# Two-scale attention and an ELU MLP on one core: batch 0 on fp16 runs, masked by TensorE; batch 1 inside block 0

## The chip, the cores and the metric

One core of a Trainium2 chip runs the whole program: TensorE (PE, matmuls), ScalarE (ACT), VectorE (DVE), GpSimd (POOL), each with its own instruction queue, worked off in order, and the queue of SyncE (SP), which issues DMAs. The metric is the device time of one execution in microseconds (us), less is better.

## The reference

Attention on q, k, v of shape 8 x 8 x 576 x 64 (batches, heads, tokens, width), twice: once with tokens averaged in fours, once with every token seeing its neighbours within 3. The sum, as 4608 tokens of 512, feeds a two-layer MLP (512 to 2048 to 512) with an ELU. The factor is 4; k and v are averaged like q.

```python
def sm_attn(qq, kk, vv):
    s = scale * np.matmul(qq, kk.transpose(0, 1, 3, 2))
    ...
    return np.matmul(a, vv)
q_d = q.reshape(B, H, Sd, factor, D).mean(axis=3)
...
out_d = sm_attn(q_d, k_d, v_d)
out_up = np.repeat(out_d, factor, axis=2)
...
mask = np.abs(pos[:, None] - pos[None, :]) < factor
scores = scale * np.matmul(q, k.transpose(0, 1, 3, 2))
scores = np.where(mask, scores, -1000000000.0)
...
return (out_up + out_local).astype(np.float32)
...
h = x @ w_in
alpha = 1.0
g = np.where(h > 0.0, h, alpha * (np.exp(np.minimum(h, 0.0)) - 1.0))
return (g @ w_out).astype(np.float32)
```

## The kernel before

**Tiling.** Attention works on a pair of heads at a time (4 pairs a batch, 8 batches), and within a pair on 6 chunks of 96 tokens; the two heads stand on partitions 0 to 63 and 64 to 127. The MLP works on 9 blocks of 512 tokens. A batch has 576 tokens, so block t needs batches up to t, and blocks 7 and 8 have no attention beside them.

**A pair.** `load` brings q by a casting DMA from GpSimd (fp32 to fp16, runs of 64 numbers) and k and v as fp32 from SP, each with a halo of 3 rows at both sides in two small DMAs. `cast` (GpSimd) makes k and v fp16. `transposes` multiplies q and k with an identity that has the means' columns beside it, so that transposed q and k and their means come from the same matmuls, and the means of v go into the same tile; ACT evicts them as qt and kt, DVE as vd and kd. `scores` makes the local scores (96 columns a chunk) and the coarse ones (two groups of 72 keys); ACT takes their exponentials (pex, dex), and DVE multiplies pex with a 0/1 mask (mex).

**A batch.** `denominators` sums mex and dex by matmuls with an indicator, DVE takes reciprocals (rc). They are spread over partitions by a write to DRAM and four reads (`spread_out`, `spread_in`, issued by ACT), in batch 0 by matmuls (`spread_pe`). `outputs` multiplies with v; DVE scales (gn, ln) and GpSimd adds the two scales into xt, the MLP's input.

**The MLP.** `mm1(t, fc)` is one of 16 groups of four matmuls of 512 columns into hp; then ACT takes exp(hp) (e), DVE min(e, 1) - 1, and DVE max(hp, 0) + e, written to gt. `mm2(t, i)` adds four matmuls to a tile op; after four of them ACT copies op to os, and SP stores it.

**Memory of results (PSUM).** 8 banks of 2 KB a partition: pool "two" (2 tiles of 2 banks: tq, tk, sc, rb, lg), pool "hp" (2 tiles of a bank) and pool "misc" (2 tiles of a bank: den, op; in blocks 0 and 1 every other hp too).

**Order.** Every call stands in a list with a time (`at`), sorted by it, and this is the order on every engine's queue. A slot is one unit of this time, with one mm1 and one mm2. `start_of` gives mm1 of block 0 slots 0 to 15, mm2 of block 0 slots 16 to 31, mm1 of block 1 slots 32 to 47; from there mm1 of block t runs beside mm2 of block t-1. Batch b starts 26.5 slots ahead of its block, with the offsets in SLOTS.

Of the kernel before, what the change touches and what calls it, by code (L numbers as in the profile page):

```python
# [12 lines left out]
AF = mybir.ActivationFunctionType  # L13

B, H, S, D = 8, 8, 576, 64
SD = S // 4
SCALE = 0.125
QB, KW, NB = 96, 102, 6
HB = 3 * QB
QW, KWW = QB + 24, 24 + KW  # L20
# [9 lines left out]
def _np_consts():  # L30

    off = np.concatenate([np.arange(96), np.arange(-3, 0), np.arange(96, 99)])
    m = np.zeros((KW, NB, QB), dtype=np.float16)
    for c in range(NB):
        for u in range(QB):
            ok = (np.abs(off - u) < 4) & (off + QB * c >= 0) & (off + QB * c < S)
            m[ok, c, u] = 1.0
    r = np.zeros((KW, 24), dtype=np.float16)
    r[np.arange(96), np.arange(96) // 4] = 0.25
    qi = np.concatenate([np.eye(96, dtype=np.float16), r[:96]], axis=1)  # L40
    ki = np.concatenate([r, np.eye(KW, dtype=np.float16)], axis=1)
    vr = np.zeros((KW, 120), dtype=np.float16)
    vr[:, 48:72] = r
    indl = np.zeros((128, 37), dtype=np.float16)
    indl[:, 5] = 1.0
    seed = np.zeros((2, 32 + HB), dtype=np.float16)
    seed[0, 6:32] = 1.0
    seed[1, 4:6] = 1.0
    seed[0, 32:] = 1.0
    seed[1, 32 + SD :] = 1.0  # L50
    sel = np.zeros((NPAIR, 32, 3, 2, 64), dtype=np.float16)
    for e in range(2):
        for g in range(2):
            sel[:, 2 * e + g, g, e] = 1.0
        sel[:, 4 + e, 2, e] = 1.0
    return m, qi, ki, vr, indl, seed, sel.reshape(128, 384)
# [12 lines left out]
def kernel(  # L69
# [13 lines left out]
    ctx.enter_context(nc.allow_low_precision("fp16 operands of TensorE"))  # L83

    def const(a, name):
        t = sb.tile(list(a.shape), FP16, tag=name, bufs=1, name=name)
        nc.sync.dma_start(out=t[:], in_=nc.inline_tensor(a, name=name + "c").ap())
        return t

    def two(name):  # L90
        return ps.tile([128, 2, 512], FP32, tag="two", bufs=2, name=name)

    m_np, qi_np, ki_np, vr_np, ind_np, seed_np, sel_np = _np_consts()
    QI, KI = const(qi_np, "QI"), const(ki_np, "KI")
    consts = {}

    def late_consts():
        consts["VR"] = const(vr_np, "VR")
        consts["MASK"] = const(m_np, "MASK")
        consts["IND"] = const(ind_np, "IND")  # L100
        consts["SEED"] = const(seed_np, "SEED")
        consts["SEL"] = const(sel_np, "SEL")

    WI = sb.tile([128, DMC, DFF], FP16, tag="WI", bufs=1, name="WI")
    WO = sb.tile([128, FCN, DM], FP16, tag="WO", bufs=1, name="WO")

    def load_weights(i):

        if i < 8:
            src = moe_w_in.rearrange("(c p) m -> p c m", p=128)[:, :, 256 * i : 256 * i + 256]  # L110
            to = WI[:, :, 256 * i : 256 * i + 256]
        else:
            n = 2 * (i - 8)
            src = moe_w_out.rearrange("(c p) m -> p c m", p=128)[:, n : n + 2, :]
            to = WO[:, n : n + 2, :]
        nc.gpsimd.dma_start(out=to, in_=src)


    st16, stT, stB, stS, stR = {}, {}, {}, {}, {}

    st32 = {}

    def load(b, j):
        q16 = sb.tile([QB, 2, NB, 64], FP16, tag="q16", bufs=5, name="q16")
        k32 = sb.tile([KW, 2, NB, 64], FP32, tag="k32", bufs=3, name="k32")
        v32 = sb.tile([KW, 2, NB, 64], FP32, tag="v32", bufs=3, name="v32")

        def rows(src, c0, nblk, tok, n):
            a = src[b, 2 * j]
            blocks = [[QB * D, 2 * NB]] if nblk == NB else [[S * D, 2], [QB * D, nblk]]  # L130
            return bass.AP(
                tensor=a.tensor, offset=a.offset + (QB * c0 + tok) * D,
                ap=[[D, n], *blocks, [1, D]],
            )

        nc.gpsimd.dma_start(out=q16[:], in_=rows(q, 0, NB, 0, QB))  # L136
        for src, dst in ((k, k32), (v, v32)):
            nc.sync.dma_start(out=dst[0:96], in_=rows(src, 0, NB, 0, QB))
            lo = 1 if (b, j) == (0, 0) else 0
            hi = NB - 1 if (b, j) == (B - 1, NPAIR - 1) else NB  # L140
            if lo or hi < NB:
                nc.gpsimd.memset(dst[96:KW, :, 0 if lo else NB - 1, :], 0.0)
            for c0, nblk, tok, p in ((lo, NB - lo, -3, 96), (0, hi, QB, 99)):
                to, a = dst[p : p + 3, :, c0 : c0 + nblk, :], rows(src, c0, nblk, tok, 3)
                if nblk == NB:
                    nc.sync.dma_start(out=to, in_=a)
                else:
                    for e in range(2):
                        nc.sync.dma_start(out=to[:, e], in_=a[:, e])
        st32[(b, j)] = (q16, k32, v32)  # L150

    def cast(b, j):
        q16, k32, v32 = st32.pop((b, j))
        k16 = sb.tile([KW, NB, 2, 64], FP16, tag="k16", bufs=2, name="k16")
        v16 = sb.tile([KW, NB, 2, 64], FP16, tag="v16", bufs=8, name="v16")
        nc.gpsimd.tensor_copy(out=k16[:], in_=k32[:].rearrange("p e c d -> p c e d"))  # L156
        nc.gpsimd.tensor_copy(out=v16[:], in_=v32[:].rearrange("p e c d -> p c e d"))  # L157
        st16[(b, j)] = (q16, k16, v16)


    def transposes(b, j):
        q16, k16, v16 = st16.pop((b, j))
        VR = consts["VR"]
        tq, tk = two("tq"), two("tk")
        for c in range(NB):
            for e in range(2):
                nc.tensor.matmul(  # L167
                    tq[64 * e : 64 * e + 64, c // 3, QW * (c % 3) : QW * (c % 3) + QW],
                    q16[:, e, c, :], QI[:], start=True, stop=True,
                )  # L170
        for c in range(NB):
            nc.tensor.matmul(  # L172
                tq[0:KG, c // 3, 3 * QW : 3 * QW + 128],
                VR[:, 48 - 24 * (c % 3) : 120 - 24 * (c % 3)], v16[:, c, :, :],
                start=(c % 3 == 0), stop=(c % 3 == 2),
            )
        qt = sb.tile([128, 2, 3 * QW], FP16, tag="qt", bufs=2, name="qt")
        nc.scalar.copy(out=qt[:], in_=tq[:, :, 0 : 3 * QW])  # L178
        vd = sb.tile([KG, 2, 128], FP16, tag="vd", bufs=8, name="vd")
        nc.vector.tensor_copy(out=vd[:], in_=tq[0:KG, :, 3 * QW : 3 * QW + 128])  # L180
        for c in range(NB):
            nc.tensor.matmul(  # L182
                tk[:, c // 3, KWW * (c % 3) : KWW * (c % 3) + KWW], k16[:, c, :, :], KI[:],
                start=True, stop=True,
            )
        tk4 = tk[:, :, 0 : 3 * KWW].rearrange("p g (c w) -> p g c w", w=KWW)
        kt = sb.tile([128, 2, 3, KW], FP16, tag="kt", bufs=2, name="kt")
        nc.scalar.copy(out=kt[:], in_=tk4[:, :, :, 24:KWW])  # L188
        kd = sb.tile([128, 2, 3, 24], FP16, tag="kd", bufs=2, name="kd")
        nc.vector.tensor_copy(out=kd[:], in_=tk4[:, :, :, 0:24])  # L190
        stT[(b, j)] = (qt, kt, kd, vd, v16)


    def scores(b, j):
        qt, kt, kd, vd, v16 = stT.pop((b, j))
        sc = [two("sc"), two("sc")]
        for c in range(NB):
            for e in range(2):
                r = slice(64 * e, 64 * e + 64)
                nc.tensor.matmul(  # L200
                    sc[e][0:KW, c // 3, QB * (c % 3) : QB * (c % 3) + QB],
                    kt[r, c // 3, c % 3, :],
                    qt[r, c // 3, QW * (c % 3) : QW * (c % 3) + QB],
                    start=True, stop=True,
                )
        for kg in range(2):
            for e in range(2):
                r = slice(64 * e, 64 * e + 64)
                qd = _free(qt[r, 0, QB : QB + 1], [[QW, NB], [1, 24]])
                nc.tensor.matmul(  # L210
                    sc[e][0:KG, kg, HB : HB + SD],
                    _free(kd[r, 0, 0, 0:1], [[1, SD]])[:, KG * kg : KG * kg + KG], qd,
                    start=True, stop=True,
                )
        pex = sb.tile([KW, 2, S], FP16, tag="pex", bufs=2, name="pex")
        dex = sb.tile([KG, 2, 2, SD], FP16, tag="dex", bufs=8, name="dex")
        for e in range(2):
            nc.scalar.activation(  # L218
# [269 lines left out]
```

## Time and profile before

| what | value |
|---|---|
| three runs | 396.29, 398.57, 398.7 us |
| median | 398.57 us |
| profiled execution, span from first to last instruction | 396.9 us |
| mean granted TensorE clock | 0.991 |
| PE busy | 354.1 us (89%), 3244 matmuls |
| DVE busy | 244.8 us (62%) |
| ACT busy | 203.8 us (51%) |
| POOL busy | 136.6 us (34%) |

For the profiled execution the page gives its span, and no time of its own; the span lies within the three runs. The page cuts the span into 40 slices of 9.9 us, with a digit for the busy tenths of each. A group's line has the source line, the engine, the operation, output and inputs, their shapes and the count; then busy us and mean ns of one; then the idle time ahead of it and what ended it. A busy PE counts the modelled end of a matmul, some 0.17 us behind the last column, so times of matmuls in a row are read from start to start.

### The profile page before, as it was taken

Reading aid. Unit: us, or ns where it says so; the run is one execution under the profiler, and the core shown is the slowest. Engines: PE = TensorE matmul, PEld = TensorE weight load, DVE = VectorE, ACT = ScalarE, POOL = GpSimd, SP = SyncE. Lnnn points to the kernel's source line nnn. Section 1 sums busy time; section 2 is a strip of 40 time slices with the busy share of each in tenths; the row PEclk is TensorE's granted clock in tenths of the full one; section 3 lists DMA queues with packets and bytes.
Section 4 is the critical chain, followed back from the end, with each engine's and each line's share of the span. In section 5 each row is a group of like instructions: output and inputs, shape, how many; then the busy total and the mean of one; then the engine's idle time right before and its main releaser. Section 6 shows DMA issues by size and latency. Waiting matters only on the chain.

```text
span 396.9 us, 8379 instructions
## 1 busy us (share of the span) xinstructions
PE 354.1 (89%) x3244; PEld 183.9 (46%) x3244; DVE 244.8 (62%) x460; ACT 203.8 (51%) x377; POOL 136.6 (34%) x184
## 2 busy tenths in 40 slices
PE   0465699996987899999999999999999899999995
PEld 0343344553544455545555554555544444444442
DVE  0123578643697976877697769766977575555510
ACT  1363158643675475657556664666375334444421
POOL 4375694402930860383038204800520040000000
PEclk9999999998998999999999999999999999999999
DMA  9899999728996892997399439906401400101112
GB/s 125 154 187 176 182 191 183 106 25 167 202 125 146 168 85 55 206 196 48 79 229 168 31 96 226 168 2 138 122 26 36 129 28 26 54 26 38 43 53 80
DMA packets 138083, 44.91 MB, mean 113 GB/s; under 512 B 122580, under 2 KB 133436, under 8 KB 138044
## 3 DMA queue, kind: packets, MB, share of 16 engines
q1 hardware_dynamic: 85644, 29.79, 31.9%
q0 software_dynamic: 43776, 8.92, 25.9%
q10 hardware_dynamic: 8624, 5.68, 6.5%
q8 instruction: 25, 0.41, 0.5%
q14 instruction: 14, 0.11, 0.1%
HBM read 43.33 MB, written 9.95 MB: 134 GB/s over the span
## 4 chain that ended last, share of the span: by engine, by line
PE 77%; DVE 6%; ACT 5%; DMA 4%; ACTq 2%; issue 2%; POOL 1%; SPq 1%; POOLq 0%; DVEq 0%
PE op L384 30%; PE hp L364 28%; PE sc L200 4%; PE tq L172 3%; PE tq L167 3%; DMA v<-in_v_dram 3%; PE lg L321 3%; DVE gt L373 2%; ACTq L272 2%; PE tk L182 2%; ACT pex L218 2%; DVE e L370 1%; DMA rd<-rc 1%; DVE mex L228 1%; POOL xt L348 1%
## 5 line engine op out<-in xcount | busy, mean ns | idle before, releaser
L364 PE MATMUL hp<-xt,WI 128*128 128x512 f16 x576 | 150.1, 388 | 2.5 <-POOL xt L348 1.4
L384 PE MATMUL op<-WO,gt 128*128 128x512 f16 x576 | 145.8, 382 | 0.0
L369 ACT ACTIVATE e<-hp 128x512 f16<-128x512 f32 x144 | 85.6, 601 | 106.2 <-PE hp L364 96.3
L373 DVE SCALAR_TENSOR_TENSOR gt<-hp,e 128x512 f16<-128x512 f32 x144 | 99.6, 692 | 5.4
L370 DVE TENSOR_SCALAR e<-e 128x512 f16<-128x512 f16 x144 | 55.9, 388 | 53.1 <-ACT e L369 52.0
L364 PEld LDWEIGHTS <-WI 128*128 128x128 f16 x576 | 54.4, 99 | 68.4 <-issue 9.3
L384 PEld LDWEIGHTS <-gt 128*128 128x128 f16 x576 | 54.4, 98 | 63.5 <-issue 1.8
L156 POOL CAST k<-k 102x768 f16<-102x768 f32 x32 | 26.8, 836 | 95.1 <-DMA k<-in_k_dram 54.0
L348 POOL TENSOR_TENSOR xt<-ln,gn 128x512 f16<-128x512 f16 (+7 forms) x64 | 42.1, 689 | 46.9 <-DVE ln L339 46.9
L218 ACT ACTIVATE pex<-sc 102x576 f16<-102x576 f32 x64 | 41.4, 647 | 21.8 <-PE sc L210 21.6
L228 DVE TENSOR_TENSOR mex<-pex,MASK 102x1152 f16<-102x1152 f16 x32 | 26.2, 817 | 38.6 <-ACT pex L218 38.4
L157 POOL CAST v<-v 102x768 f16<-102x768 f32 x32 | 29.7, 927 | 37.3 <-DMA v<-in_v_dram 37.2
L178 ACT CAST qt<-tq 128x720 f16<-128x720 f32 x32 | 24.3, 758 | 35.3 <-PE tq L172 31.2
L390 ACT COPY os<-op 128x512 f32<-128x512 f32 x36 | 21.2, 588 | 19.9 <-PE op L384 19.9
L200 PE MATMUL sc<-qt,kt 64*102 64x96 f16 x384 | 18.9, 224 | 12.9 <-ACT kt L188 7.2
L180 DVE CAST vd<-tq 72x256 f16<-72x256 f32 x32 | 13.4, 417 | 27.5 <-ACT qt L178 26.5
L136 POOL DMA_DIRECT2D q<-in_q_dram x32 | 28.6, 893 | 3.9 <-DMA WI<-in_moe_w_in_dram 3.0
L167 PE MATMUL tq<-QI,q 96*64 96x120 f16 x384 | 17.4, 230 | 10.4 <-DMA q<-in_q_dram 5.9
L200 PEld LDWEIGHTS <-kt 64*102 64x102 f16 x384 | 14.0, 132 | 27.1 <-ACT kt L188 13.2
L222 ACT ACTIVATE dex<-sc 72x288 f16<-72x288 f32 x64 | 25.8, 404 | 0.0
L172 PE MATMUL tq<-v,VR 102*72 102x128 f16 x192 | 18.0, 234 | 7.0 <-POOL v L157 7.0
L339 DVE TENSOR_TENSOR ln<-lg,rcb 128x576 f16<-128x576 f32 x32 | 23.9, 746 | 0.0
(35 smaller groups left out, 211.9 us busy)
## 6 DMA issues: line engine op xcount, KB each, us to landing
k<-in_k_dram SPq DMA_DIRECT2D x32, 288.0 KB
v<-in_v_dram SPq DMA_DIRECT2D x32, 288.0 KB
out_dram<-os SPq DMA_DIRECT2D x36, 256.0 KB
q<-in_q_dram POOLq DMA_DIRECT2D x32, 144.0 KB, 4.5
rcb<-rd ACTq DMA_DIRECT2D x14, 288.0 KB
WI<-in_moe_w_in_dram POOLq DMA_DIRECT2D x8, 256.0 KB, 10.8
WO<-in_moe_w_out_dram POOLq DMA_DIRECT2D x8, 256.0 KB, 9.3
rcb<-rd ACTq DMA_DIRECT2D x14, 72.0 KB
```

Source lines behind the costliest of these rows:

```text
L157: nc.gpsimd.tensor_copy(out=v16[:], in_=v32[:].rearrange("p e c d -> p c e d"))
L167: nc.tensor.matmul(tq[64 * e : 64 * e + 64, c // 3, QW * (c % 3) : QW * (c % 3) + QW], q16[:, e, c, :], QI[:], start=True, stop=True,)
L172: nc.tensor.matmul(tq[0:KG, c // 3, 3 * QW : 3 * QW + 128], VR[:, 48 - 24 * (c % 3) : 120 - 24 * (c % 3)], v16[:, c, :, :], start=(c % 3 = ...
L200: nc.tensor.matmul(sc[e][0:KW, c // 3, QB * (c % 3) : QB * (c % 3) + QB], kt[r, c // 3, c % 3, :], qt[r, c // 3, QW * (c % 3) : QW * (c % ...
L218: nc.scalar.activation(out=pex[:, e, :].rearrange("p (g u) -> p g u", g=2), in_=sc[e][0:KW, :, 0:HB], func=AF.Exp, scale=SCALE,)
L228: nc.vector.tensor_tensor(out=mex[:], in0=pex[:], in1=mk2, op=AB.mult)
L348: nc.gpsimd.tensor_tensor(out=xt(t)[:, j, t0 - TBLK * t : t1 - TBLK * t], in0=ln[:, a:z], in1=_rep4(gn[:, a // 4 : z // 4]), op=AB.add,)
L364: nc.tensor.matmul(hp[:], WI[:, dc, 128 * fc : 128 * fc + 128], x[:, dc, :], start=(dc == 0), stop=(dc == DMC - 1),)
L369: nc.scalar.activation(out=e[:], in_=hp[:], func=AF.Exp)
L370: nc.vector.tensor_scalar(out=e[:], in0=e[:], scalar1=1.0, scalar2=-1.0, op0=AB.min, op1=AB.add)
L373: nc.vector.scalar_tensor_tensor(out=gts[t][:, fc, :], in0=hp[:], scalar=0.0, op0=AB.max, in1=e[:], op1=AB.add)
L384: nc.tensor.matmul(op_[:], gts[t][:, fc, 128 * tt : 128 * tt + 128], WO[:, fc, :], start=(fc == 0), stop=(fc == FCN - 1),)
```

## The change

**Batch 0** (`first_batch`, written out in order). q and k come by eight casting DMAs from GpSimd in runs of six tokens (1536 bytes of fp32), so that chunk c holds tokens 6r + c, and the eviction puts them in order by a strided read. The mask is added by TensorE: a matmul of an identity with -30000 or 0 goes into the scores' bank first. The means of q and k are reductions on DVE. The denominators are made in two halves of two pairs each (`den_half`), and spread by matmuls.

**Later batches.** q and k stay fp32, come from SP, are transposed as fp32 by TensorE, and evicted as fp16; their sums over four tokens are two steps of additions on GpSimd each. v comes with its halo in one DMA of 112 rows.

`den_half` has two seeds, 24 matmuls of 96 columns and 8 of 144; a half goes on with the sums of v, the spread and the outputs of its two pairs.

**Order.** mm1 of block t runs in slots 16t to 16t+15, mm2 of block t one block later, from block 0 on. Batch 1's attention stands within block 0, its outputs at slot 15.9. The loads of W_out are issued behind batch 0's outputs, those of W_in among batch 0's casts of v.

**PSUM.** The pools "hp" and "misc" are replaced by two tiles of two banks, duo0 and duo1. From block 1 on hp is one of duo0's halves in turn, op and den one of duo1's; in block 0 hp goes duo0, duo1, duo0, duo1. In batch 0 they hold the scores, half of the denominators and outputs.

```diff
+    duo = [ps.tile([128, 1024], FP32, tag=f"duo{i}", bufs=1, name=f"duo{i}") for i in range(2)]
...
+    def bank(i, n=512):
+        return duo[i // 2][:, 512 * (i % 2) : 512 * (i % 2) + n]
+
+    def misc_bank():
+        misc[0] += 1
+        return bank(2 + misc[0] % 2)
...
     def denominators(b):
-        den = ps.tile([128, 512], FP32, tag="misc", bufs=2, name="den")
+        den = misc_bank()
...
     def mm1(t, fc):
-        tag = "misc" if t < 2 and fc % 2 else "hp"
-        hp = ps.tile([128, TBLK], FP32, tag=tag, bufs=2, name="hp")
+        hp = bank((0, 2, 1, 3)[fc % 4]) if t == 0 else bank(fc % 2)
...
     def mm2(t, i):
-            ops[t] = ps.tile([128, DM], FP32, tag="misc", bufs=2, name="op")
+            ops[t] = misc_bank()
...
+    def load_qk(b, j):
+        for src, name in ((q, "q"), (k, "k")):
+            a = src[b, 2 * j]
+            if b == 0:
+                t = sb.tile([QB, 2, TPP * D], FP16, tag=name + "in", bufs=4, name=name + "16")
+                nc.gpsimd.dma_start(
+                    out=t[:],
+                    in_=bass.AP(
+                        tensor=a.tensor, offset=a.offset,
+                        ap=[[TPP * D, QB], [S * D, 2], [1, TPP * D]],
+                    ),
+                )
+            else:
+                t = sb.tile([QB, NB, 2, D], FP32, tag=name + "in", bufs=4, name=name + "32")
+                for e in range(2):
+                    nc.sync.dma_start(
+                        out=t[:, :, e, :],
...
...
+    def transposes(b, j):
...
+                if b == 0:
+                    for e in range(2):
+                        nc.tensor.matmul(
+                            t[64 * e : 64 * e + 64, 128 * c : 128 * c + QB],
+                            x[:, e, D * c : D * c + D], C["NI"][0:QB, 0:QB],
+                            start=True, stop=True,
+                        )
                 else:
+                    a = 512 * (c // 3) + QB * (c % 3)
+                    nc.tensor.transpose(
+                        t[:, a : a + QB], x[:, c, :, :].rearrange("p e d -> p (e d)"), C["I32"][:]
+                    )
...
+    def sums(b, j, x):
...
+        if b == 0:
+            nc.vector.tensor_reduce(
+                out=to[:], in_=src.rearrange("p (g f) -> p g f", f=4), axis=AX.X, op=AB.add
+            )
+        else:
+            two_ = sb.tile([128, 2 * SD], FP32, tag="t2", bufs=2, name="t2")
+            at_ = src.rearrange("p (g f) -> p f g", f=2)
+            nc.gpsimd.tensor_tensor(out=two_[:], in0=at_[:, 0], in1=at_[:, 1], op=AB.add)
+            at_ = two_[:].rearrange("p (g f) -> p f g", f=2)
+            nc.gpsimd.tensor_tensor(out=to[:], in0=at_[:, 0], in1=at_[:, 1], op=AB.add)
...
+    def den_half(b, h, den):
...
+        rc = RC[(b, h)] = sb.tile([64, SD], FP16, tag="rch", bufs=2, name="rch")
+        nc.vector.reciprocal(out=rc[:], in_=den[0:64, 0:SD])
...
+    def first_batch():
...
+        for j in range(NPAIR):
+            for e in range(2):
+                scores(b, j, e, duo[e], True)
+            if j < 3:
+                transposes(b, j + 1)
+            exp_local(b, j, 0, duo[0])
+            exp_local(b, j, 1, duo[1])
+            for e in range(2):
+                coarse(b, j, e, duo[e])
...
+            exp_coarse(b, j, 0, duo[0])
...
+                sums(b, j + 1, "q")
+                sums(b, j + 1, "k")
+                load_qk(1, j + 1)
...
+        for h in range(2):
+            dv = two("dv") if h == 0 else duo[0]
+            den_half(b, h, dv)
...
+                v_sums(b, 2 * h + i, dv[0:KG, 512 + 256 * i : 768 + 256 * i], 128)
...
+                copy = act if h == 1 else dve
+                spread_copy(b, j, rbs[j], copy, copy)
...
+                outputs(b, j, lg)
+                normalise(b, j, lg)
+        for n in range(8):
+            load_wo(n)
...
+        if b == 1:
+            tr, sc_ = (1, 2.5, 5.5, 8.5), (4, 7, 10, 11.5)
+            base, d0, s0, s1, o0 = 0, 12.6, 13, 13.4, (15.9, 15.95)
+        elif b == 2:
+            base = 12
+            tr, sc_ = (0, 1.6, 4.8, 8), (3.2, 6.4, 9.6, 11.2)
+            d0, s0, s1, o0 = 12.8, 13.6, 14.6, (17.6, 18.4)
         else:
-            base = start_of(b) - 26.5
+            base = 16 * b - 25
+            tr, sc_ = (0, 1.6, 4.8, 9.7), (3.2, 6.4, 11.3, 12.9)
+            d0, s0, s1, o0 = 14.5, 16.1, 17.1, (21, 22.6)
...
     for t in range(NT):
         for s in range(16):
-            at(start_of(t) + s + 0.25, mm1, t, s)
-            at((16 if t == 0 else start_of(t + 1)) + s + 0.75, mm2, t, s)
+            at(16 * t + s + 0.25, mm1, t, s)
+            at(16 * (t + 1) + s + 0.75, mm2, t, s)
```

## The prediction

> **What bounds the kernel now.** I read the page's slices, then the timeline of a stretch without attention (330 to 345 us), then the chain of waits to 135 us, then the windows there. The page:
>
> ```profile
> span 396.9 us, 8379 instructions
> PE   0465699996987899999999999999999899999995
> PEclk9999999998998999999999999999999999999999
> L364 PE MATMUL hp<-xt,WI 128*128 128x512 f16 x576 | 150.1, 388 | 2.5 <-POOL xt L348 1.4
> L384 PE MATMUL op<-WO,gt 128*128 128x512 f16 x576 | 145.8, 382 | 0.0
> ```
>
> TensorE starts the MoE at about 50 us (slices 0 to 4 are half empty) and is full from 150 us on. The span lies inside the measured 396.29 to 398.7 us (median 398.57), so under 2 us lie around it; the sum is made against 396.9. One step of a paired stage, from the timeline (start, length, engine):
>
> ```profile
> 335.82 1.03 PE L364 MATMUL hp<-xt,WI 128*128 128x512 f16 x4
> 336.68 1.03 PE L384 MATMUL op<-WO,gt 128*128 128x512 f16 x4
> 336.88 0.60 ACT L369 ACTIVATE e<-hp 128x512 f16<-128x512 f32 x1 [1.13 <-PE hp L364]
> 337.51 0.29 DVE L370 TENSOR_SCALAR e<-e 128x512 f16<-128x512 f16 x1 [0.71 <-ACT e L369]
> 337.54 1.03 PE L364 MATMUL hp<-xt,WI 128*128 128x512 f16 x4
> 337.84 0.69 DVE L373 SCALAR_TENSOR_TENSOR gt<-hp,e 128x512 f16<-128x512 f32 x1
> ```
>
> mm1 and mm2 take 0.86 us each (335.82 to 336.68 to 337.54), a step 1.72. The ELU of the same mm1 ends at 338.53, 2.71 us after its start, and the next mm1 starts 0.99 us before that. It may, because two hp tiles alternate. This overlap is the row to remember. From the chain of waits (start, length), the marks of the first stages:
>
> ```profile
> 35.50 1.02 PE den L244 x13
> ...
> 49.63 7.33 PE hp L364 x21
> ...
> 84.72 3.45 DMA rd<-rc
> ...
> 118.45 1.61 DMA rd<-rc
> ```
>
> The first rows end batch 0 and start the MoE, the last two are the DRAM write of the denominators on the critical chain.
>
> **The change part by part.** *The hp banks.* In the new code hp is no longer a pool of two tiles but a half of one tile, duo0 (blocks 1 to 8), and op and den are halves of duo1. The built program keeps its waits by tile: every mm1 of blocks 1 to 8 (128 of them, and 2 of block 0) waits for the gt of the mm1 just before it; in the old program nearly all wait for one at least two back (142 of 144). So the step becomes mm1's start to gt's end, 2.71, plus 0.05 from DVE to PE (vd ends at 110.29, scores start at 110.34): 2.76 us. mm2 and most attention then lie inside it. Alone this makes 128 x 2.76 = 353 us.
>
> *Attention on top of 2.76*, for a full block (block 4, with parts of batches 5 and 6). Price of a pair's transposes: 12 matmuls of 96 columns, fp32, of which the trace has no row. Bounds: 36 ns (fp16 q transposes, 12 in 0.43 us) and 216 ns (a 512-column matmul); I take 55, from the k transposes with 128-column weights (6 in 0.33 us), so 0.66, with 0.37 for v's sums and 0.1 of entry about 1.2 us, as before (1.21). Other rows: scores 0.63, outputs of two pairs 0.98, denominators 1.05, pex and dex 0.65 and 0.40, evictions 0.65 each, rc 1.95, gn and ln 1.05 a pair, mask 0.82.
> Transposes between mm1 and mm2 (2 steps): PE 0.86 + 1.2 + 0.86 = 2.95 with its entry, +0.2 each. Transposes behind mm2: the two evictions run 3.1 to 4.4 and hold the next e, ready at 2.95 + 1.06 = 4.0, by 0.4: +0.6. Scores between mm1 and mm2: nothing, their four exps end at 3.8, when the next e is ready. Scores behind mm2 (2 steps): exps end at 4.6 against 3.82: +0.8 each. Transposes with outputs in one step: outputs need the two buffers that the evictions free at 4.2 and 4.4, PE ends at 5.1: +2.4. Scores with outputs: outputs wait for the exps (2.7 and 3.8), mm2 ends at 5.16: +2.4. Denominators: rc queues behind gt (2.71 to 4.66) and reads duo1, so mm2, which writes duo1's other half, waits for it and ends at 5.57: +2.8. The four DMA issues of spread_in (2.6 us on ACT, 120.09 row) hold an e by 0.4. Sum 0.4 + 0.6 + 0 + 1.6 + 2.4 + 2.4 + 2.8 + 0.4 = 10.6, a block 44.2 + 10.6 = 54.8 us (the trace of before: about 38.2, 16 x 1.72 + 10.5 of attention). Block 1 is 55.9 by the same list and about 1 us wait for xt; blocks 2 to 5 54.8; block 6 (half a batch) 49.1; 7 and 8 have none, 44.2. Together 412.6 us.
>
> *Startup.* q and k of batch 0 in 1536-byte runs: 192 packets a DMA for 1152; Pool issues 8 at 0.71 (WO's row, 256 packets) to 0.89 (q's). The first q landed at 5.88; I put k's at 6.5 and the first scores at 8.3. The masks (mex, 0.82 on DVE) become two 288-column matmuls a head, the sums two reductions on DVE (0.75, the row of 576 elements) beside ACT's work. A pair then costs 5.1 at the slow clock of the startup (scores with the mask 2.0, exps and evictions 0.65 each on ACT in turn); before, 5.36 (21.17 to 26.53) from 13.2 on. The pair after pair chain ends at 26.9 instead of 35.5, but the halves (den_half, rc about 1.0, v's sums, spread, outputs, normalise) run one behind the other, 8.3 us to the second den_half and about 10 from it to the last xt: first full mm1 at about 45 against 49.6. The strided eviction has no row; if it took twice 0.65, 8 x 0.65 = 5 us are lost, if halves overlap 5 are won.
>
> *Block 0 with batch 1.* Its mm1s alternate duo0 and duo1 and keep their overlap. Pool first issues eight WO loads (0.71 each, 5.7 us), then casts v: v's sums of the first pair end near 7.4 us. Behind that each pair needs two buffers for transposes, evictions, scores, exps: 5.5 us, so the masks end at 29, den 32, rc 34, the DRAM write 36.5 (1.61 to 3.45 in the chain), four ACT issues 39, landing 42, four normalises and xt 48. mm1 of block 1 stands in PE's queue ahead of mm2 of block 0 and waits for all of it; before, mm2 of block 0 covered it. So 45 + 48 = 93; block 0, mm2 alone and all before mm1 of block 1 ended at 103.6 before.
>
> *Rest.* Pool per pair: k's cast (0.84) and q's issue (0.89) go, sums come: two of 288 (between the 256 and 320 rows, 0.69) and two of 144 (0.44), 2.26. Scores stand 3.2 slots behind, 8.8 us at 2.76, so they are hidden; without that cover up to 2.26 a pair. kd's copies (0.30 on DVE) go, not on the path. SP issues q too, past which k, v and stores queue, but a batch, some 50 us, ahead of use, against 4.5 to 13.5 us to land. Tail: mm2 of block 8, 64 x 0.216 = 13.8; each next op waits for os (0.24 + 0.59 + 0.05) three times, 2.6; os and the store 4 (393 to 396.9): 20.4.
>
> **Sum.** 93 + 412.6 + 20.4 = 526; after each den step PE idles 2.8 us, as it did before 124.75 (shown below), where the granted clock fell; one slow step each, 0.9 x 6: about 531.
>
> **The rivals.** *Clock.* A pure step leaves PE idle 1.0 of 2.76 us. Two gaps of before on PE, and windows over and behind them (start and end, length, PE busy, granted clock, DMA share, GB/s):
>
> ```profile
> 110.34 0.65 PE L200 MATMUL sc<-qt,kt 64*102 64x96 f16 x12 [1.40 <-DVE vd L180]
> ...
> 124.75 0.65 PE L200 MATMUL sc<-qt,kt 64*102 64x96 f16 x12 [2.80 <-DVE vd L180]
> ```
>
> ```profile
> 108.00:112.00 4.00, 2.58 (x27) 1.00 1.56 170
> ...
> 128.00:132.00 4.00, 4.00 (x49) 0.74 0.93 201
> ```
>
> The 1.40 us gap left the clock at 1.00, behind the 2.80 one it fell. The startup, busy some 60%, ran scores in 1.01 us that later took 0.48, though its slices read 9. If steps fall to that half rate, e starts 0.9 later, 3.65 a step; PE is then 95% busy and recovers, so at most about half of them: 64 x 0.9 = 58, 589 us. The Trainium skill, TensorE: Matmul & The Clock Gate (A second HAM failure mode: psum-queue depth-cycling), describes this: short idles between groups of matmuls make the clock swing between half and full. By that rule the time is the 589; the 110.34 row speaks against it, no steady row is like it. Chance 0.12.
> *fp32 transposes slow.* At 160 ns, towards the 216 end, 12 cost 1.92, +1.26 in 24 of the pairs: 561 us. Chance 0.12. The Trainium skill, TensorE: Matmul & The Clock Gate (LDWEIGHTS), puts a load at columns over 1.2 in ns, an estimate of 107 ns for 128 columns, 546 us. The score rows load 102 columns twelve times in 0.32 us on two row groups, 53 ns each where the rule gives 85, so I stay at 55.
> *Faster.* The wait on gt costs nothing, PE stays the bound: 93 for the start, then PE's work alone: 1088 matmuls of the MoE by 0.216 make 235, six batches by 10.5 make 63, less 3 for what stands in block 0, and 4 for the last store: 392 us, without the stalls that before has in its stages of mm1 or mm2 alone. It decides if mm1's start to gt's end falls under 2.39, the mean step of a full block now. It is 2.71 with nothing in its way. That the banks' waits aren't on the chip is the same case: 0.04.
> *Attention hides better* than listed, half of the extras: 500 us; part of the forecast's range.
>
> **How the numbers follow.** Forecast 0.72, 531 us, its own range 495 to 565 (extras 64 by half or more, startup and block 0 plus or minus 10). The wide range takes in the two slow cases: 492 to 585. A measurement here tells 1% apart. Faster 0.04; within 1% 0.01, the strip between; slower the rest, 0.95.
>
> **What would show it.** Of the changed profile: between two mm1s of blocks 7 and 8 2.76 us, with gt of DVE as what ended PE's idle time; the PE slices at 6 to 7 tenths there instead of 9; mm2 behind den held by rc; the first mm1 at 40 to 50 us; PEclk full in blocks 7 and 8 (else the clock rival); the fp32 transposes under 0.1 us each start to start. Wrong if PE is full in blocks 7 and 8.

## The result, and the profile after

| | median us | range | runs |
|---|---|---|---|
| before | 398.5 | 396.29 to 398.7 | 4 |
| after | 540.05 | 537.79 to 542.88 | 4 |

The changed kernel takes 1.356 times the time (95% interval 1.351 to 1.362). Ratios, unlike medians, leave out slow executions: four of before, one of f1 (424.94 us) and one of e8, which took 922.54 us with matmuls of 0.83 us in place of 0.39. The profiled execution has a span of 538.5 us. Its page, with the span, two rows of slices (13.5 us each) and the two groups of the MLP's matmuls:

```profile
span 538.5 us, 8199 instructions
...
PE   4875966877886867776686778776766766676676
...
PEclk9999996899799999989999999899999999999999
...
L454 PE MATMUL duo<-xt,WI 128*128 128x512 f16 x576 | 155.5, 392 | 92.3 <-DVE gt L463 86.6
...
L474 PE MATMUL duo<-WO,gt 128*128 128x512 f16 x576 | 150.4, 388 | 16.5 <-DVE rc L333 13.7
```

The matmuls' own time hardly changed (155.5 and 150.4 us, 150.1 and 145.8 before). What is new is behind the second bar: ahead of mm1 TensorE sat idle for 92.3 us, 86.6 of them for gt, where it was 2.5; ahead of mm2 16.5, 13.7 of them for rc, where it was 0. The last slices, which hold nothing but mm1 and mm2, are busy 6 to 7 tenths instead of 9. A step there, from the timeline (start, length, engine):

```profile
471.42 1.02 PE L454 MATMUL duo<-xt,WI 128*128 128x512 f16 x4 [0.88 <-DVE gt L463]
...
472.27 1.03 PE L474 MATMUL duo<-WO,gt 128*128 128x512 f16 x4
472.48 0.60 ACT L459 ACTIVATE e<-duo 128x512 f16<-128x512 f32 x1 [2.17 <-PE duo L454]
...
473.11 0.29 DVE L460 TENSOR_SCALAR e<-e 128x512 f16<-128x512 f16 x1 [1.74 <-ACT e L459]
...
473.43 0.69 DVE L463 SCALAR_TENSOR_TENSOR gt<-duo,e 128x512 f16<-128x512 f32 x1
...
474.18 1.02 PE L454 MATMUL duo<-xt,WI 128*128 128x512 f16 x4 [0.87 <-DVE gt L463]
```

The durations are those of before; their order in time is not. mm1 starts at 471.42, its exponential at 472.48, the last step of the ELU ends at 474.12, and only then, at 474.18, does the next mm1 start, though it writes the other half of duo0. One step is 2.76 us, where two hp tiles let it be 1.72. mm2 fills part of the wait and 0.87 us stay empty.

The places of the blocks on the time axis say where the time went. These are starts of the first matmul of each block's first mm1, read from the timelines, and the lengths from one to the next; a full block is one of blocks 2 to 5, with a whole batch of attention beside it, and blocks 7 and 8 have none. The other rows are the experiments below.

| kernel | block 2 starts | blocks 2, 3, 4, 5 | block 6 | block 7 | span |
|---|---|---|---|---|---|
| before | 135.2 | 39.1 38.3 38.3 38.3 | 34.6 | 27.6 | 396.9 |
| after | 153.9 | 57.3 57.3 55.2 56.8 | 49.4 | 44.3 | 538.5 |
| e1_four_tiles | 142.0 | 44.1 42.7 43.0 43.3 | 34.7 | 27.6 | 422.6 |
| e2_hp_apart | 143.6 | 47.8 46.8 45.8 46.5 | 37.2 | 27.7 | 444.2 |
| e3_misc_apart | 151.6 | 54.9 53.0 53.1 53.4 | 46.8 | 44.3 | 517.9 |
| e4_before_one_hp | 133.3 | 50.8 48.7 48.5 48.4 | 47.0 | 44.3 | 482.2 |
| e6_old_spacing | 145.7 | 43.6 44.1 44.4 39.6 | 35.4 | 27.6 | 425.8 |
| e9_spread_on_sp | 144.4 | 39.1 39.1 39.1 39.1 | 33.8 | 27.6 | 407.6 |
| f1_old_order | 140.7 | 43.9 44.0 43.9 39.6 | 35.6 | 27.6 | 420.6 |
| g1_before_new_batch0 | 131.9 | 38.7 38.6 38.3 38.3 | 34.6 | 27.6 | 393.3 |

From block 2 on every block is longer by 15 to 19 us, those without attention too; block 2 starts 18.7 us later, and the tail from the start of the last mm1 grew by 3.1 (22.8 and 19.7).

### The profile page after: what moved, and what is told of

Read it like the earlier page. It is cut to its first block, busy times and chain, and to the rows that moved or that the text cites. A ratio compares the mean times of both kernels' runs of the same rounds, so it can differ in the third digit from the quotient of the medians.

```text
span 538.5 us, 8199 instructions
## 1 busy us (share of the span) xinstructions
PE 391.8 (73%) x3164; PEld 208.0 (39%) x3164; DVE 233.5 (43%) x431; ACT 201.9 (37%) x377; POOL 143.3 (27%) x241
## 4 chain that ended last, share of the span: by engine, by line
PE 45%; DVE 24%; ACT 17%; issue 5%; ACTq 3%; POOL 3%; DMA 3%; DVEq 0%; POOLq 0%
PE duo L454 21%; DVE gt L463 11%; PE duo L474 11%; ACT e L459 9%; DVE e L460 6%; ACTq L346 3%; ACT pex L278 3%; DVE rc L333 3%; PE tk L199 2%; ACT dex L283 2%; PE tq L199 2%; PE lg L411 2%; DMA rd<-rc 2%; DVE mex L293 2%; PE tq L240 1%
## 5 line engine op out<-in xcount | busy, mean ns | idle before, releaser
L454 PE MATMUL duo<-xt,WI 128*128 128x512 f16 x576 | 155.5, 392 | 92.3 <-DVE gt L463 86.6
L459 ACT ACTIVATE e<-duo 128x512 f16<-128x512 f32 x144 | 86.0, 599 | 241.9 <-PE duo L454 232.2
L474 PE MATMUL duo<-WO,gt 128*128 128x512 f16 x576 | 150.4, 388 | 16.5 <-DVE rc L333 13.7
L454 PEld LDWEIGHTS <-WI 128*128 128x128 f16 x576 | 54.9, 99 | 172.6 <-issue 115.9
L463 DVE SCALAR_TENSOR_TENSOR gt<-duo,e 128x512 f16<-128x512 f32 x144 | 99.6, 692 | 5.4
L278 ACT ACTIVATE pex<-sc 112x576 f16<-112x576 f32 x56 | 36.2, 647 | 8.4 <-PE sc L593 7.6
L212 ACT CAST qt<-tq 128x576 f16<-128x576 f32 x32 | 20.4, 638 | 36.7 <-PE tq L240 32.6
L293 DVE TENSOR_TENSOR mex<-pex,MASK 112x1152 f16<-112x1152 f16 x28 | 21.9, 782 | 25.1 <-ACT pex L278 25.1
L480 ACT COPY os<-duo 128x512 f32<-128x512 f32 x36 | 21.1, 586 | 22.6 <-PE duo L474 22.6
L181 POOL CAST v<-v 112x768 f16<-112x768 f32 x32 | 27.2, 864 | 6.9 <-DMA v<-in_v_dram 6.7
L218 ACT CAST kt<-tk 128x576 f16<-128x576 f32 x32 | 20.6, 644 | 0.1
L199 PE MATMUL tq<-I,q 96*128 96x96 f32 x168 | 19.7, 256 | 1.1 <-ACT dex L283 1.1
```

Source lines behind the costliest of these rows:

```text
L181: nc.gpsimd.tensor_copy(out=v16[:], in_=v32[:].rearrange("p (e c) d -> p c e d", e=2))
L199: nc.tensor.transpose(t[:, a : a + QB], x[:, c, :, :].rearrange("p e d -> p (e d)"), C["I32"][:])
L278: nc.scalar.activation(out=h2(s["pex"][:, e, :]), in_=g2(sc[0:KW], 0, HB), func=AF.Exp, scale=SCALE)
L293: nc.vector.tensor_tensor(out=s["mex"][:], in0=s["pex"][:], in1=mk2, op=AB.mult)
L454: nc.tensor.matmul(hp, WI[:, dc, 128 * fc : 128 * fc + 128], x[:, dc, :], start=(dc == 0), stop=(dc == DMC - 1),)
L459: nc.scalar.activation(out=e[:], in_=hp, func=AF.Exp)
```

## The experiments

Theory A, the prediction's: the two waits by tile, for gt and for rc, cost most of the 141 us. Its rival B: another part of the change does.

**Which tile costs what (e1 to e4).** In e1 the four banks are given back behind batch 0 and taken anew as four tiles:

```diff
-    duo = [ps.tile([128, 1024], FP32, tag=f"duo{i}", bufs=1, name=f"duo{i}") for i in range(2)]
+    early = ctx.enter_context(ExitStack())
+    psd = early.enter_context(tc.tile_pool(name="psd", bufs=1, space=bass.MemoryType.PSUM))
+    duo = [psd.tile([128, 1024], FP32, tag=f"duo{i}", bufs=1, name=f"duo{i}") for i in range(2)]
+    def four_tiles():
+        early.close()
+        late["ps"] = ctx.enter_context(tc.tile_pool(name="psl", bufs=1, space=bass.MemoryType.PSUM))
...
     def misc_bank():
-        misc[0] += 1
-        return bank(2 + misc[0] % 2)
+        return late["ps"].tile([128, 512], FP32, tag="misc", bufs=2, name="misc")[:]
+    def hp_bank():
+        return late["ps"].tile([128, 512], FP32, tag="hp", bufs=2, name="hp")[:]
...
-        hp = bank((0, 2, 1, 3)[fc % 4]) if t == 0 else bank(fc % 2)
+        hp = misc_bank() if t == 0 and fc % 2 else hp_bank()
```

> The changed kernel, with hp, op and den of blocks 0 to 8 in four tiles of one bank each (two for hp, two for op and den) in place of the halves of duo0 and duo1; batch 0 keeps duo0 and duo1, whose banks are given back behind it. All instructions and their order stay. Theory A (the waits by tile cost the time): the step of blocks 7 and 8 falls from 2.76 to 1.72 us, a block from 44.2 to 27.6; mm1 of block 1 stays at 94 us; 94 + 6 blocks of about 38 + 33 + 2 x 27.6 + a tail of 18 make about 396 us, 385 to 412. Theory B (another part of the change costs it: fp32 transposes, sums on GpSimd, the new order, the clock): most of the 141 us stay, above 480 us.

Measured 422.41 us, 1.060 (1.055 to 1.066) times before. 118 of the 141 us go with the tiles alone, and blocks 7 and 8 are back at 27.6 us. But the expected 396 is missed by 26: full blocks take 42.7 to 44.1 us, not 38, and that is not the tiles.

e2 makes only op and den halves of one tile again, as shown; e3 does the same with hp alone:

```diff
+        if "misc" not in late:
+            late["misc"] = late["ps"].tile([128, 1024], FP32, tag="misc", bufs=1, name="misc")
+            late["n"] = 0
+        late["n"] += 1
+        return late["misc"][:, 512 * (late["n"] % 2) : 512 * (late["n"] % 2) + 512]
```

> As the kernel with four tiles, but op and den are again halves of one tile; only hp has two tiles. Theory A, as the prediction prices it: mm2 behind each of seven den steps waits for rc (up to 2.8 us less what mm1 covers, 1.5 to 2.8 each, 10 to 20 in all), a next op waits for os (28 times 0 to 0.6 us), the tail +2.6: 12 to 35 us above the kernel with four tiles, about 410 to 430. Theory C (the shared tile of op and den is the main cost): above 480 us.

> As the kernel with four tiles, but hp is again two halves of one tile; op and den have two tiles. Theory A: step 2.76 us in blocks 7 and 8 as in the changed kernel; the waits of mm2 for rc and for os go, so 540 less 7 x 1.5 to 2.8 and less 2.6 in the tail: 515 to 530 us. Theory C: below 460 us.

Measured 444.73 us (1.114, 1.107 to 1.121) and 519.09 (1.303, 1.296 to 1.310). What TensorE waited for (total, times, longest), in e2 and in e3:

```profile
PE misc L484 <- DVE rc L343: 13.7, 6, 2.5
...
PE misc L484 <- ACT os L490: 2.9, 4, 0.7
PE misc L464 <- DVE rc L343: 2.8, 1, 2.8
```

```profile
PE hp L464 <- DVE gt L473: 86.1, 100, 1.8
```

The two costs can be had apart and they add: the half tile of hp costs 95.3 us with op and den shared (540.05 - 444.73) and 96.7 without (519.09 - 422.41), that of op and den 21.0 and 22.3. Both differences lie in theory A's ranges; e2's 410 to 430 us was missed by what e1 already had too much. C falls.

e4 puts the shared tile into the kernel of before; hps[1] is one tile of two banks, taken at the start of block 2:

```diff
-        hp = ps.tile([128, TBLK], FP32, tag=tag, bufs=2, name="hp")
+        if t < 2:
+            hp = (ps if tag == "misc" else hps[0]).tile([128, TBLK], FP32, tag=tag, bufs=2, name="hp")
+        else:
+            hp = hps[1][:, fc % 2, :]
```

> The kernel of before, in which hp of blocks 2 to 8 is two halves of one tile of two banks in place of two tiles; nothing else changes. Theory A: blocks 7 and 8 go from 27.6 to 44.2 us, blocks 2 to 6 from about 38 to about 53: 7 blocks by 15 to 17 us, 398 + 105 to 119 = 503 to 517 us. Theory B (the shared tile alone costs little, it needs the new order or the new transposes): below 430 us.

Measured 485.03 us (1.217, 1.210 to 1.223): 86 us for the tile alone, with no other part of the change. Blocks 7 and 8 take 44.3 (44.2 put); blocks 2 to 5 take 48.4 to 50.8 where 53 was put, so 18 to 32 us of the sum are missing. The attention of before adds 4.2 us to a block of 44.3 (blocks 3 to 5), that of the change (e3) 8.9. So a part of attention's price belongs not to the tile but to the change's attention; its order, its transposes and its sums all differ, and these two runs do not tell them apart.

**The 23 us that are not tiles (e5 to e7).** In a full block of e1 (228.8 to 271.8 us) TensorE waited for:

```profile
PE lg L417 <- ACT dex L292: 1.3, 2, 1.1
PE lg L417 <- DVE vd L581: 1.2, 1, 1.2
PE sc L592 <- ACT kt L227: 1.1, 1, 1.1
```

3.6 us, at the outputs that stand right behind the next batch's transposes or scores and need their buffers. In the same stretch of before (212.6 to 250.9) nothing is listed. Three suspects, each alone in e1, in this order: e5 brings q and k as fp16, with two casting DMAs each, and transposes them as fp16; e6 takes the spacing of before; e7 spreads the eight loads of W_out on GpSimd.

```diff
+            elif b >= 2:
+                t = sb.tile([QB, NB, 2, D], FP16, tag=name + "in", bufs=4, name=name + "16")
+                for e in range(2):
+                    nc.gpsimd.dma_start(
+                        out=t[:, :, e, :],
...
+                    nc.tensor.matmul(
+                        t[:, a : a + QB], x[:, c, :, :], C["NI"][0:QB, 0:QB],
+                        start=True, stop=True,
+                    )
```

```diff
-            base = 16 * b - 25
-            tr, sc_ = (0, 1.6, 4.8, 9.7), (3.2, 6.4, 11.3, 12.9)
-            d0, s0, s1, o0 = 14.5, 16.1, 17.1, (21, 22.6)
+            base = 16 * b - 26.5
+            tr, sc_ = (0, 3.2, 9.7, 12.9), (1.6, 4.8, 11.3, 14.5)
+            d0, s0, s1, o0 = 16.1, 17.7, 18.7, (22.5, 24.1)
```

```diff
-        for n in range(8):
-            load_wo(n)
...
+    for n in range(8):
+        at(3 + 1.4 * n, load_wo, n)
```

> As the kernel with four tiles, but q and k of batches 2 to 7 come as fp16 by casting DMAs from GpSimd (four a pair in place of four of SP) and are transposed as fp16 by a matmul with the identity. The twelve fp32 transposes took 82 ns each from start to start; fp16 rows with weights of the same width took 55 (before) or less. Theory D (their excess lies on the path): 24 pairs by 12 x 27 to 40 ns = 8 to 12 us less than 422, 410 to 415. Theory E (the excess of the order over the kernel before has another place): 419 to 424. If the issues on GpSimd hold up its sums, above 424.

> As the kernel with four tiles, but batches 3 to 7 have the spacing of the kernel before (transposes at 0, 3.2, 9.7, 12.9, scores 1.6 behind each, outputs at 22.5 and 24.1, base 26.5 ahead), so that no outputs stand right behind transposes or scores of the next batch. A full block of the kernel with four tiles took 42.3 to 43.3 us against 38.3, and PE idled 3.65 us of it at four places, all waiting for evictions or exps to free a buffer. Theory F (these collisions are what the order costs): 5 blocks by 3 to 3.65 us less, 404 to 408. Theory G (coarse scores then wait for GpSimd's sums, which are done only 4.6 us behind the start of the transposes, or the fp32 transposes are the cost): 416 to 424.

> As the kernel with four tiles, but the eight loads of W_out are not issued in a row behind batch 0's outputs: they stand 1.4 slots apart from slot 3 on, behind the first casts of v of batch 1. PE sat idle for 4.29 us at 47.9, until GpSimd had issued the eight (5.7 us) and cast v. Theory H (that wait is on the path to mm1 of block 1): 3 to 5 us less, 417 to 420. Theory I (the chain of batch 1 has other waits that take its place): 421 to 424.

*e5* measured 430.55 us (1.080, 1.073 to 1.086), 8 more than e1 and not 8 to 12 less. Six transposes now take 0.26 us from start to start (210.24 to 210.50), 43 ns each, but blocks 3 to 5 stay at 42.7 to 43.2 (42.7 to 43.3 in e1). In block 4 TensorE's busy time falls by 1.6 us (39.25 to 37.65) and its idle time grows by as much, 1.1 of it a new wait for v. Block 2 starts 7.7 us later, since four issues a pair on GpSimd hold up its casts of v:

```profile
PE tq L265 <- POOL v L200: 13.0, 9, 4.2
```

In e1 this was 4.3 us, once. So the case that was put for GpSimd held up by its issues, above 424, is the one that came. Theory D is not borne out, but a run that brings a wait of its own does not refute it either.

*e6* measured 426.53 us (1.070, 1.065 to 1.075), so G's number came out, but not G's reason. The three collisions are gone, and each of blocks 2 to 4 has a new stop. Its timeline:

```profile
209.85 0.59 ACTq L352 DMA_DIRECT2D rcb<-rd  x1
...
210.49 0.36 SPq L488 DMA_DIRECT2D out_dram<-os  x1
210.49 4.98 ACTq L352 DMA_DIRECT2D rcb<-rd  x3
...
210.94 1.19 SPq L151 DMA_DIRECT2D q<-in_q_dram  x2
...
212.22 1.19 SPq L151 DMA_DIRECT2D k<-in_k_dram  x2
...
214.19 0.92 SPq L167 DMA_DIRECT2D v<-in_v_dram  x1
215.51 0.60 ACT L465 ACTIVATE e<-hp 128x512 f16<-128x512 f32 x1 [5.05 <-DMA rcb<-rd]
...
217.22 1.02 PE L460 MATMUL hp<-xt,WI 128*128 128x512 f16 x4 [2.97 <-DVE gt L469]
```

The four reads of spread_in are issued by ACT, in 5.6 us here; in e1 they took 2.6. In those 5.6 us SP issues five loads. ACT's next exponential waits behind the issues, its gt behind that, and mm1 2.97 us for gt. Block 5 has no loads to issue, since batch 8 does not exist; there the reads took 2.6 us and the block 39.6. This led to theory J: the two queues' issues hold each other up. What holds the fourth read is looked up below, behind e9.

*e7* measured 419.57 us (1.052, 1.046 to 1.057): 2.8 us less than e1 and inside H's 417 to 420, at its edge. The intervals of e1 and e7 overlap, so the gain is not clear of the noise. Block 2 started 5.0 us earlier and block 2 itself took 1.6 more.

**A move that moved nothing, and one that did (e8, e9, f1, g2).** f1 takes over the whole order of the kernel before (start_of, spacing) behind the new batch 0, and issues the loads of W_out 1.9 slots apart:

```diff
+    tr, sc_ = (0, 3.2, 9.7, 12.9), (1.6, 4.8, 11.3, 14.5)
...
+        base = start_of(b) - 26.5
...
+            at(start_of(t) + s + 0.25, mm1, t, s)
+            at((16 if t == 0 else start_of(t + 1)) + s + 0.75, mm2, t, s)
```

> Batch 0, loads, transposes and sums of the changed kernel, four tiles, W_out 1.9 slots apart, and the order of the kernel before (mm2 of block 0 alone, then mm1 of block 1 alone, its spacing). Theory: the first mm1 comes at about 44 instead of 46.4 to 49.6; from there on as before, with up to 0.5 us a pair for the fp32 transposes: 392 to 402 us. Rival: the sums on GpSimd hold up the coarse scores, which stand 1.6 slots behind the transposes, by 0.7 us a pair: 405 to 415.

Measured 422.94 us (1.054, 1.043 to 1.066), neither range. Its trace shows two reasons. The coarse scores wait for GpSimd's sums, 11.0 us in 12 places, 10.0 us of it in 9 places before block 2, where the steps are short. And three full blocks have the same stop as e6 (43.9 to 44.0 us, 39.6 in the one without loads). To test J I issued the second pair's loads later, in e6 (e8) and in f1 (g2):

```diff
-                at(base + tr[j] + 0.05, loads, b + 1, j)
+                at(base + tr[j] + (2.25 if j == 1 else 0.05), loads, b + 1, j)
```

> As the kernel with four tiles and the old spacing (426.5 us), but the five loads of the second pair of the next batch are issued 2.25 slots behind its transposes instead of 0.05, so behind the issues of spread_in. There, ACT issued the four reads of rcb in 5.6 to 5.8 us in the three blocks in which SP issued these loads at the same time, and in 2.6 in the one without loads, which took 39.6 us against 43.6 to 44.4. Theory J (the two queues' issues hold each other up, and e and the evictions wait behind them on ACT): spread_in 2.6 us everywhere, those three blocks 39.6 to 40.5, 412 to 416 us. Theory G (the block without loads is short because it has less traffic, or GpSimd's sums are the cost): above 422.

> The same single move of the loads in the kernel that has batch 0 and the transposes and sums of the changed kernel, four tiles and the order of the kernel before (422.9 us). Theory J: three blocks of 44 go to 39.6 to 40.5, 408 to 413 us. Theory G: above 419.

Measured 427.69 us (1.078, 1.064 to 1.091) and 420.6 (1.060, 1.047 to 1.073): no gain. But this is no evidence against J, since the edit did nothing. The only trace of e8 is that of the 922.54 us, so g2 shows it: SP issues q at 205.84, as soon as the transposes that start at 205.06 free the buffer, in the midst of ACT's reads (204.53 to 209.82), as in f1. A place in the list sets the order on one queue; SP had nothing else to do, and no place on another queue holds it back. So e9 puts the four reads into SP's own queue, in e6:

```diff
     def spread_in(b):
...
-                nc.scalar.dma_start(
+                nc.sync.dma_start(
```

> As the kernel with four tiles and the old spacing (426.5 us, not the two with moved loads), but the four reads of rcb are issued by SP in place of ACT. The loads' move before this one moved nothing: SP had no other work, so it issued them as soon as their buffers were free, at the same time as ACT its reads, as before. Theory J (ACT is held 5.6 to 5.8 us by its issues beside SP's, and e, evictions and mm1 wait behind it): PE's idle time of 2.97 to 3.32 us ahead of an mm1 that waits for gt goes from three blocks, and with it the dip of the clock; those blocks go from 43.6 to 44.4 to 39.6 to 40.5 us, 412 to 416 us. Theory G (traffic or GpSimd's sums): above 422.

Measured 408.73 us (1.028, 1.022 to 1.035), better than J's range. SP's queue in the same block, and TensorE and the clock (start and end, length, then busy time of PE, PEld, DVE, ACT and POOL, granted clock, DMA share, GB/s) in e9 and, behind its stop, in e6:

```profile
205.10 2.57 SPq L352 DMA_DIRECT2D rcb<-rd  x4
207.77 1.10 SPq L151 DMA_DIRECT2D q<-in_q_dram  x2
```

```profile
180.00:220.00 40.00, 39.87 (x373) 22.46 (x372) 28.40 (x51) 23.40 (x45) 18.06 (x30) 1.00 0.69 141
```

```profile
217.00:225.00 8.00, 7.51 (x68) 3.57 (x68) 5.06 (x12) 4.24 (x9) 1.91 (x4) 0.79 0.58 88
```

All four full blocks are 39.1 us. So the held ACT was the price, and G falls: traffic and GpSimd's sums are the same in e6 and e9. Each against its own runs of before, e1 is 23.3 us slower and e9 10.8. Some 12 us of e1's 23 were thus the place of attention and of the four reads, as collisions in e1 and as a held ACT in e6. What is left of e9 stands ahead of block 2, which starts at 144.4 instead of 135.2, and in 0.8 us in each of blocks 3 to 5, 0.2 a pair.

How ACT is held is not as J says. Each of its reads in e6 takes 0.58 to 0.65 us to issue, no longer than alone; the 5.6 us have 3.1 us of nothing in them, between the third read (211.15 to 211.79) and the fourth (214.88). The trace shows what the fourth waits for. Each DMA of the two queues tells its landing by one of eight semaphores (counters that engines wait on), and an issue waits until the DMA that had its semaphore before has landed. The fourth read has that of the output store that SP issued at 210.49, and the store landed at 214.86. In block 2 of e6 the profile names the store itself, as what ended ACT's idle time:

```profile
171.63 0.60 ACT L465 ACTIVATE e<-hp 128x512 f16<-128x512 f32 x1 [4.85 <-DMA out_dram<-os]
```

In all nine stops of e6, f1 and g2 the fourth read starts 0.02 us after the landing of a store that SP had issued 3.7 to 4.7 us before. In the full blocks of e1 that have loads (2 to 4) the DMA that had its semaphore before had landed 1.5 to 1.7 us earlier, in those of e9 4.8 to 6.2, so nothing waited. No run changed the semaphores alone: this is read from the traces, and e9 takes the wait off ACT whatever its cause.

The Trainium skill, Perfetto Trace Analysis (DMA Instruction — HWDGE (DVE, Sync)), names another way for two queues to hold each other: the sequencers of DVE and Sync share one block that generates descriptors, one at a time locks it, and the wait for the lock is part of the profiled length. For ACT the trace does not bear this out, since its issues kept their length. SP's five loads did grow beside ACT's reads, from 2.33 us (0.86, 1.01 and 0.46) to 3.30; by what, no run tells.

**A version a little faster than before (g1).** Batch 0 and its loads from the changed kernel, everything from batch 1 on (load, cast, transposes, scores, order) from the kernel before, four tiles:

```diff
     for b in range(1, B):
...
+        base = start_of(b) - 26.5
...
+            at(base + (SLOTS[2 * j - 2] if j else -3.1) + 0.1, cast, b, j)
...
+            at(base + SLOTS[2 * j], pair_transposes, b, j)
+            at(base + SLOTS[2 * j + 1], pair_scores, b, j)
```

> Batch 0 and its loads from the changed kernel; everything from batch 1 on from the kernel before (casting loads, fp16 transposes with the means' columns, order, spacing), hp, op and den in four tiles. If the new batch 0 is worth what its first mm1 shows (42 to 44 against 46.4 to 49.6 us) and the rest is as before: 392 to 396 us. If batch 1, whose loads come later now, takes the gain back: 398 to 402.

Measured 395.78 us (0.994, 0.990 to 0.998; ten runs, 393.36 to 397.81, against 399.06). This is in the range that was put for a new batch 0 that keeps its gain. Block 2 starts 3.3 us earlier and the blocks behind it are as before within 0.4 us. That is the part of the change worth keeping, and it is small: 0.6%, clear of its interval, but less than the spread of single runs.

## Why the prediction was right

Forecast 531 us, measured 540.05, span 538.5. The step that carries the forecast, mm1 waiting for the gt just before it, is shown below; that the total came so near is in part luck. The sum without its 5.4 us for slow steps was 526, 12.5 short of the span: 7.4 in blocks 2 to 5, 3.5 in block 0, 2.7 in block 1, less 1.2 in the startup. The slow steps stood in for part of that.

*The hp banks, 2.76 us a step.* Measured 2.76; blocks 7 and 8 44.3 us (44.2 put). Waiting for gt is what ends the idle time, as it said. e3 against e1 and e4 against before show it as the cause: 97 and 86 us.

*Attention's extras, 10.6 us a block.* 12.4 came, the mean of blocks 2 to 5 (56.65) less 44.2; block 6 49.4 (49.1 put). The den step, priced 2.8, took 2.1 to 4.3 a block (after less e3, waits for os included). The two collisions of outputs, priced 4.8, were not measured alone. The one term known to be mis-sized is the transposes' price, 55 ns a matmul. Measured from the timeline of after:

```profile
234.62 0.70 PE L199 MATMUL tq<-I,q 96*128 96x96 f32 x6
235.16 0.66 PE L199 MATMUL tk<-I,k 96*128 96x96 f32 x6
235.66 0.50 PE L240 MATMUL tq<-v,VR 112*72 112x128 f16 x6
```

Six take 0.50 us (235.16 to 235.66) to 0.54: at 83 ns, twelve cost 0.34 us more than put, 1.4 a block of four pairs, if all of it is on the path; 1.8 are missing. That it is on the path was not shown, and in e5 faster transposes shortened no block by more than 0.6 us. The 83 ns lie between the 36 and 216 ns of the bounds; the forecast took a row of fp16 where the work was fp32. The Trainium skill, TensorE: Matmul & The Clock Gate (LDWEIGHTS), makes such a load an estimate of 107 ns; the trace lies between that rule and my row.

*Startup and block 0.* First mm1 on a full xt at 43.83 (45 put). The first mm1 of block 1 starts at 92.20 and has its full xt at 95.32 (93 put), so block 0 took 51.5 us for 48. The chain of waits after has the links that it named: eight loads of W_out ahead of the first cast of v, rc, the DRAM write, and the last xt.

```profile
44.03 5.70 POOL WO L120 x8
...
77.23 1.87 DVE rc L333
79.12 1.98 DMA rd<-rc
...
90.49 4.79 POOL xt L438 x7
```

*Block 1.* 58.6 us (95.32 to 153.89) for 55.9, the largest miss of one block. Two of its slices show the clock at 8 and 7 tenths; it was at half from 142.6 to 149.3. How much of the 2.7 is the clock was not tried alone.

*Rest.* One slow step behind each of six den steps was put at 0.9 us. From block 2 on there are five, each with an idle time of 2.5 us ahead of mm2. Behind three of them (173.1, 230.4 and 342.9 us) the clock was 0.79 over the next 8 us, behind two (287.7 and 399.7) 1.00. The tail from the end of the last gt, 518.40, is 20.1 us (20.4 put).

*The rivals.* Clock: two windows of the stages without attention, which idle 0.9 us in each 2.76 (columns as above):

```profile
440.00:474.00 34.00, 22.80 (x97) 9.31 (x96) 12.64 (x26) 9.51 (x16) 0.00 (x0) 1.00 0.06 23
474.00:518.00 44.00, 30.20 (x128) 12.40 (x128) 15.50 (x33) 11.65 (x20) 0.00 (x0) 1.00 0.06 24
```

Full clock throughout, at 67 and 69% busy. The rule of the Trainium skill, TensorE: Matmul & The Clock Gate (A second HAM failure mode: psum-queue depth-cycling), that short idles between groups of matmuls make the clock swing, does not hold for these. fp32 transposes at 160 ns: not so. "Faster", 392 us, if the waits cost nothing: e1 has 1.0 us of waits for gt left and takes 422. That rival's sum counted TensorE's work alone; it left out the collisions (3.6 us a block) and put nothing for waits within block 1.

## What to carry to other kernels

A wait is kept by tile: two buffers that are halves of one tile are one buffer, and a double-buffered loop over them runs at its chain's latency, here 2.76 us for 1.72. Price an order by the buffers and queues at each step, not by its engines' sums: attention's place and the queue of four reads cost some 12 us that showed as collisions in one order and as a held ACT in the next. ACT sat idle for 4.85 us over four issues of its own: look up what an issue waits for, here the landing of another queue's store on the same semaphore. A later place in the list delays a DMA only against what stands in its own queue.

## What the runs showed of the hardware

- ACT's four reads took 2.6 us to issue in e1, and 5.6 to 5.8 in the three blocks of e6 in which the fourth waited for the landing of SP's output store, which had its semaphore. Issued from SP's queue they took 2.57 (e9), and the loads behind them went on at once.
- Gaps of TensorE of 0.9 us in every 2.76 left the clock at 1.00 for 78 us (after, 440 to 518). Behind five of 2.5 us it was 0.79 over the next 8 us three times and 1.00 twice (after); behind one of 2.97 us it was 0.79 (e6).
- An fp32 transpose of 96 x 128 takes 83 ns from start to start; as fp16, by a matmul with the identity, 43 (e5).
